# Attention on two lanes of 64 array rows, projections in halves, one PV run a unit

## The chip, the cores and the metric

The kernel runs on one core of a Trainium2 chip. TensorE multiplies (PE in the profile, PEld its weight loads), VectorE (DVE), ScalarE (ACT) and GpSimd (POOL) work on what it leaves, and SyncE (SP) starts the DMAs. Every engine takes its instructions in the order in which they were issued and waits for others by semaphores. The metric is the device time of one execution in microseconds; before, three runs gave a median of 1934.09 us (1932.29 to 1937.3).

## The reference

Two layers, each of an attention with a compressive memory and a gated feed-forward part, on x of 2048 rows and 512 columns. Cut to what matters:

```python
q, k, v = heads(x @ wq), heads(x @ wk), heads(x @ wv)   # 32 heads of 16, 4 segments of 512 rows
for s in range(4):
    logits = einsum("qd,kd->qk", qs, ks) * 0.25 + causal_mask
    a_dot = softmax(logits) @ vs
    a_mem = (phi(qs) @ M) / (phi(qs) @ z + 1e-6)        # phi(t) = t + 1 if t > 0 else exp(t)
    outs.append(g * a_mem + (1 - g) * a_dot)
    M, z = M + phi(ks).T @ vs, z + phi(ks).sum(rows)
x = x + concat(outs) @ wo                               # on layernorm(x)
x = x + (silu(h @ w_gate) * (h @ w_up)) @ w_down        # h = layernorm(x)
```

## The kernel before

The whole program is a list of operations. Each names its engine, a modelled cost, what it reads and writes, and a due time (`P.prio`, set by `at`). `Program.issue` (L148) then walks through modelled time and issues, on each engine, the due operation with the earliest due time whose inputs are there. So the order in every engine's queue is fixed when the kernel is built, by the planner's costs (`LAT`, `DRAIN`), its due times (`OFF`, `PRE`, `EP`) and the pitch of a unit (`TA`, `TF`). SyncE's queue is ordered in the same way.

Matrices are fp32r, one pass of the array. To keep precision the projections and the feed-forward part split each operand in a high and a low half and multiply three combinations (`mm3`, L285): 12 matmuls of 512 columns with 128 contraction rows for each 128x512 result. Its matmuls have line L282. PV, the memory and the transposes are plain fp32.

Attention runs over 32 units a layer: segment s, group n of eight heads, half h of four heads. For a unit:

- `load3` (L490) brings q and k of four heads from DRAM into `cq` and `ck`. The 48 contraction rows of a head (16 high, 16 low, 16 high) stand in a full-height operand among zeros.
- `mx_units` (L518): for each head the logits by query in groups of 256 + 256, 384 and 512 columns (L531). VectorE takes the maximum of each row (L538). `fin` transposes the maxima (L547), ScalarE negates them and a DMA writes them into `cq` as another contraction row (L550), so that the next product already has the maximum subtracted.
- `at_units` (L560): `lt` makes the logits by key, for two head pairs at once, ten tiles of 2 x 256 columns (L575). ScalarE takes the exp out of PSUM (L581), GpSimd masks the diagonal tiles (L585). `pv` multiplies with v on four lanes of 32 array columns (L603), in two runs. `post` drains (L616 to L637) and adds the part of the memory, whose transposes are L630.

Around this stand the projections of the next groups (`qk_proj`, `v_proj`, `wo_proj`), the layer norm with its transposes (`ln_transpose`, L370), phi (L475 to L480: Relu and Exp on ScalarE, the sum on VectorE), the reading of the memory (`mem_read`, L645) and its update (`mem_update`, L665, another run on column lanes). In the last units of a layer the first tiles of its feed-forward part are worked in (`up`, `down` and `ln` for blocks 0 and 1). The rest of that part works by Strassen's scheme (L987) and by `down` (L1042).

PSUM has eight banks, fixed by use: two `pmx` for maxima, three `plt` for the logits by key, one `ppv`, and two `pj` for all the rest, given out by the planner.

Of the kernel before, what the change touches and what calls it, by code (L numbers as in the profile page):

```python
# [26 lines left out]
WOT = ("pmx_0", "pmx_1", "pj", "pj")  # L27
# [4 lines left out]
WQ1 = -6.0  # L32
TA, TF = 15.0, 16.7
OFF = {'qe': (0.481, 1.468), 'at': (0.3, 1.1), 'mx': (-0.666, 0.16), 'lf': (-0.709, -0.318), 'mr': (0.865, 0.781), 'mu': (0.556, 0.139), 'wo': (0.263, 1.746), 'qk': (-0.342, 0.41), 'v': (-0.3, 0.518), 'lp': (0.034, 1.108)}
PRE = {'c': -1.851, 'mb': 0.212, 'lv': -1.7, 'lo': -0.87, 'gate': -1.0, 'v': -1.534, 'dv': 0.12, 'qk1': -1.2, 'mx': -1.0}
EP = {'w': -1.935, 'wn': 0.178, 'ln': -3.0, 'dn': -0.06, 'up': -2.73}
POOL_W = ""
TABLE = 1.28
DRAIN = {("full", "cols"): 0.195, ("cols", "full"): 0.095}
# [3 lines left out]
    pe=dict(pe=0.01, act=0.2, dve=0.2, sp=0.19),  # L43
# [7 lines left out]
class Buf:  # L51
    def __init__(self, prog, pool, tag, shape, dtype):
        self.prog, self.pool, self.tag, self.shape, self.dtype = prog, pool, tag, shape, dtype
        self.ops, self.left = [], 0
        self.w, self.r = {}, {}
        self.tile = None
        self.slot = None
# [10 lines left out]
class Op:  # L68
    __slots__ = ("table", "mode", "post", "eng", "cost", "lat", "fn", "prio", "bufs", "succ", "deps", "ready", "need", "wait", "index")

    def __init__(self, eng, cost, lat, fn, prio, bufs):
        self.eng, self.cost, self.lat, self.fn, self.prio, self.bufs = eng, cost, lat, fn, prio, bufs
        self.mode, self.table, self.post = None, None, 0.0
        self.succ, self.deps, self.ready, self.need, self.wait = [], set(), 0.0, None, 0


class Program:
# [3 lines left out]
    def __init__(self, shared):  # L81
        self.shared = shared
# [14 lines left out]
    def op(self, eng, cost, fn, reads=(), writes=(), lat=0.0):  # L97
# [38 lines left out]
        for b in touch:  # L136
# [3 lines left out]
            if b.tag in self.shared:  # L140
                o.need = b
# [6 lines left out]
    def issue(self):  # L148
        for b in {id(b): b for o in self.ops for b in o.bufs if b.tag in self.shared}.values():
# [9 lines left out]
        engs = sorted({o.eng for o in self.ops})  # L159
# [5 lines left out]
        held = {tag: [] for tag in self.shared}  # L165
        for o in self.ops:
            if o.wait == 0:
                heapq.heappush(fut[o.eng], (o.ready, o.index, o))
        done, bus, table, mode = 0, 0.0, "exp", "full"
        while done < len(self.ops):  # L170
            best = None
            for e in engs:
                f, n = fut[e], now[e]
                while True:
# [3 lines left out]
                    if n:  # L178
                        o = n[0][2]
                        b = o.need  # L180
                        if b is not None and b.slot is None:
                            if not free[b.tag]:
                                heapq.heappop(n)
                                held[b.tag].append(o)
                                continue
                            fr = min(free[b.tag])
# [5 lines left out]
                        start = t[e]  # L192
                    elif f:
                        start = f[0][0]
                        if best is None or start < best[0]:
                            t[e] = start
                            continue
                    else:
                        start = None
                    break  # L200
                if start is not None and n and (best is None or start < best[0]):
                    best = (start, e)
            assert best is not None, "no instruction can issue"
            start, e = best
            n = now[e]
            o = n[0][2]
            heapq.heappop(n)
            b = o.need
            if b is not None and b.slot is None:
                fr = min(free[b.tag])  # L210
                free[b.tag].remove(fr)
                b.slot = fr[1]
# [13 lines left out]
            end = t[e] + o.post  # L226
            if o.lat:
                bus = max(bus, end + 0.65) + o.lat
                end = bus
            for b in o.bufs:  # L230
                b.left -= 1
                if b.left == 0 and b.slot is not None:
                    free[b.tag].append((end + 0.25, b.slot))
                    for w in held[b.tag]:
                        w.ready = max(w.ready, end + 0.25)
                        heapq.heappush(fut[w.eng], (w.ready, w.index, w))
                    held[b.tag] = []
            for s in o.succ:
                s.ready = max(s.ready, end + LAT[e].get(s.eng, 0.0))
                s.wait -= 1  # L240
                if s.wait == 0:
                    heapq.heappush(fut[s.eng], (s.ready, s.index, s))
# [3 lines left out]
def infini_swiglu(ctx: ExitStack, tc: tile.TileContext, x, wq, wk, wv, wo, beta, wg, wu, wd, out,  # L246
# [8 lines left out]
    P = Program({"pj": 2})  # L255
# [5 lines left out]
    def bank(tag, ring=1):  # L261
        return P.buf(psum, tag, [128, 512], F32, ring)

    def pe(n, passes, fn, reads, writes, loads=1, mode="full"):
        o = op("pe", max(passes * n / 2400 + 0.0025 + 0.0145 * loads * (passes == 1), 0.11 * loads), fn, reads, writes)
        o.mode = mode
# [25 lines left out]


# [3 lines left out]
    amask = sb("amask", [128, 512], BF16)  # L297
    bsel = sb("bsel", [128, 4, 2])
# [71 lines left out]
    def ln_transpose(xn, xh, xl, t, tag="pj"):  # L370
        ps = bank(tag)
        for kc in range(KC):
# [6 lines left out]
            [ps, (xh, t)], [(xl, t)])  # L379

# [11 lines left out]
    SG = ("Y", "raw")  # L392

    CK = {}

    def attention(lay, x_in, x_out, slots, T, hook):
# [40 lines left out]
        def ln_fin(s, t, tag="pj"):  # L437
            if t == 0:
                xT[s] = (sb(S8["xh"], TX, F32R), sb(S8["xl"], TX, F32R))
            ln_transpose(XN.pop((s, t)), xT[s][0], xT[s][1], t, tag)  # L440

        def v_proj(s, t, tag="pj"):
            if s < 2 and t == 0:
# [5 lines left out]
            ps = bank(tag)  # L449
            c = slice(t * 128, (t + 1) * 128)  # L450
            mm3(ps, xT[s], W["v"], range(KC), lambda a, kc: a[:, t, kc], lambda a, kc: a[:, kc, :],
                lambda kc: t, lambda kc: kc, "a")
            vt = VT[s % 2]
# [4 lines left out]
        def qk_proj(s, n, nm, tag="pj"):  # L458
# [3 lines left out]
            ps, nat = bank(tag), g["nat"]  # L462
            a = 0 if nm == "q" else 1
            c = slice(n * 128, (n + 1) * 128)
            mm3(ps, W[nm], xT[s], range(KC), lambda t, kc: t[:, kc, c], lambda t, kc: t[:, :, kc],
                lambda kc: kc, lambda kc: None, "b")
# [739 lines left out]
```

## Time and profile before

| | before |
|---|---|
| median of three runs | 1934.09 us |
| the profiled execution | 1932.95 us |
| its span in the trace | 1931.2 us |
| granted TensorE clock, mean | 0.994 |
| layer 1: drains of the PV results, first to last | 77.6 to 534.3 us |
| layer 2: the same | 1037.9 to 1491.1 us |

The profile's page gives busy time by engine, the span in forty slices, the chain that ended last, and groups of instructions by line and tile. In a row of groups stand line, engine, operation, output and inputs, then the shapes and the count, then busy time and mean duration of one in ns, then the engine's idle time before them and what ended it. Matmuls are pipelined: one that starts 0.24 us after another may be shown as 0.4 us long. A row of windows has the stretch, its length, the busy time of each engine with its instructions, the granted clock, and the DMA engines' share and GB/s. A row of the timeline has start, length, engine, line, what is done, and how often in a row.

### The profile page before, as it was taken

To read this page: it belongs to the slowest core of one execution; us is meant where nothing else is said; L and a number is where in the kernel's file an instruction comes from. 1 tells how busy PE (TensorE), PEld (TensorE's weight loads), DVE (VectorE), ACT (ScalarE), POOL (GpSimd) and SP (SyncE) were. 2 spreads that over 40 slices of the span, in tenths; PEclk is the share of its full clock that TensorE was granted. 3 is DMA by queue.
4 is the path that set the end of the run, shared out by engine and by line. 5 is a ranking of instruction groups with operands and counts; after the bars stand their busy time and mean duration, and the time that the engine had idled before them with its cause. 6 is when DMAs were issued, how large, how long until landed. Compare 5 with 4: busy or idle time off the path is not lost.

```text
span 1931.2 us, 32319 instructions
## 1 busy us (share of the span) xinstructions
PE 1870.8 (97%) x11104; PEld 1437.2 (74%) x11104; DVE 1406.9 (73%) x3834; ACT 873.0 (45%) x1634; POOL 905.9 (47%) x1185
## 2 busy tenths in 40 slices
PE   7999999999989999999999999999999999999999
PEld 5677677776668887788867777777766788878887
DVE  5877867778777668766777678777797756686656
ACT  4555454555624343334326555555455334333332
POOL 5333443444546553655534334444355365455461
PEclk9999999999999999999999999999999999999999
DMA  7433434456131122221364344344561321221121
GB/s 235 135 111 124 132 116 146 129 151 195 45 136 50 55 72 82 71 61 44 95 215 121 102 133 132 116 149 132 152 188 39 131 66 44 87 77 51 44 60 44
DMA packets 120819, 206.09 MB, mean 107 GB/s; under 512 B 14160, under 2 KB 43856, under 8 KB 120656
## 3 DMA queue, kind: packets, MB, share of 16 engines
q1 hardware_dynamic: 118608, 203.49, 34.8%
q8 instruction: 89, 1.46, 0.3%
q10 hardware_dynamic: 2048, 0.53, 0.1%
q14 instruction: 74, 0.61, 0.1%
HBM read 136.34 MB, written 67.11 MB: 105 GB/s over the span
## 4 chain that ended last, share of the span: by engine, by line
PE 78%; DVE 8%; issue 4%; DMA 4%; POOL 3%; ACT 2%; SPq 0%; ACTq 0%; DVEq 0%; POOLq 0%
PE pj L282 16%; PE pj L1049 14%; PE plt L1005 11%; PE pmx L531 8%; PE pmx L1005 8%; PE ppv L603 7%; PE plt L575 6%; PE ppv L1005 3%; DVE junk L538 2%; DMA ck<-scrk 1%; PE pj L975 1%; PE pj L373 1%; PE pj L653 1%; DMA s<-nm 1%; POOL mem L858 1%
## 5 line engine op out<-in xcount | busy, mean ns | idle before, releaser
L538 DVE CUSTOM_DVE_ANT_0 junk<-pmx,amask 128x128 bf16<-128x128 f32 (+3 forms) x1024 | 458.7, 484 | 116.9 <-PE pmx L531 112.0
L282 PE MATMUL pj<-s,s 128*128 128x512 f32 x1416 | 488.2, 410 | 4.9 <-DVE s L1054 4.5
L1049 PE MATMUL pj<-s,vt 128*128 128x512 f32 x1296 | 414.4, 398 | 7.1 <-DVE s L1054 4.5
L581 ACT ACTIVATE s<-plt 128x512 f32<-128x512 f32 x512 | 284.2, 601 | 141.3 <-PE plt L575 133.3
L282 PEld LDWEIGHTS pj<-s,s 128*128 128x128 f32 x1416 | 263.9, 190 | 71.4 <-issue 24.9
L531 PE MATMUL pmx<-ck,s 127*128 127x256 f32 (+2 forms) x1024 | 299.1, 347 | 16.9 <-DVE mx L538 9.5
L1005 PE MATMUL plt<-s,s 128*128 128x512 f32 x1008 | 296.2, 396 | 3.4 <-ACT tt L1020 2.3
L1049 PEld LDWEIGHTS pj<-s,vt 128*128 128x128 f32 x1296 | 243.5, 189 | 68.9 <-DVE s L1054 8.0
L1054 DVE TENSOR_TENSOR s<-s,pj 128x512 f32<-128x512 f32 x224 | 152.9, 684 | 137.9 <-PE pj L1049 137.7
L575 PE MATMUL plt<-s,ck 128*128 128x256 f32 x1280 | 241.6, 288 | 4.2 <-DMA s<-nm 2.1
L531 PEld LDWEIGHTS pmx<-ck,s 127*128 127x128 f32 x1024 | 178.7, 190 | 88.8 <-DVE mx L538 27.0
L1005 PE MATMUL pmx<-s,s 128*128 128x512 f32 x720 | 239.2, 396 | 3.6 <-ACT s L871 2.4
L575 PEld LDWEIGHTS plt<-s,ck 128*128 128x128 f32 x1280 | 211.2, 189 | 32.7 <-ACT s L581 8.5
L1005 PEld LDWEIGHTS plt<-s,s 128*128 128x128 f32 x1008 | 189.6, 189 | 50.4 <-ACT tt L1020 2.7
L585 POOL TENSOR_SCALAR_AFFINE_SELECT s<-s 128x512 f32<-128x512 f32 x192 | 126.9, 664 | 186.5 <-ACT s L581 180.1
L1005 PEld LDWEIGHTS pmx<-s,s 128*128 128x128 f32 x720 | 135.5, 189 | 36.4 <-ACT s L871 3.2
L603 PE MATMUL ppv<-s,vt 128*32 128x512 f32 (+2 forms) x1536 | 136.8, 458 | 0.0
L872 POOL TENSOR_TENSOR s<-mem,s 128x512 fp32r<-128x512 f32 x96 | 126.4, 1318 | 0.0
L469 POOL TENSOR_SCALAR s<-raw 128x512 fp32r<-128x512 f32 x64 | 39.9, 624 | 181.0 <-ACT raw L468 180.6
L1005 PE MATMUL ppv<-s,s 128*128 128x512 f32 x288 | 112.8, 394 | 0.0
L879 POOL COPY turn<-vt 128x1 f32<-128x1 f32 x20 | 3.7, 184 | 230.0 <-DVE vt L962 230.0
L581 ACT ACTIVATE pc<-plt 128x512 f32<-128x512 f32 x128 | 76.8, 600 | 63.8 <-PE plt L575 62.5
(197 smaller groups left out, 2872.5 us busy)
## 6 DMA issues: line engine op xcount, KB each, us to landing
s<-scrq SPq DMA_DIRECT2D x128, 192.0 KB, 3.5
ck<-scrk SPq DMA_DIRECT2D x128, 192.0 KB, 4.5
scrq<-s SPq DMA_DIRECT2D x32, 512.0 KB, 3.0
scrk<-s SPq DMA_DIRECT2D x32, 512.0 KB, 3.1
scrq<-s SPq DMA_DIRECT2D x32, 256.0 KB, 2.0
scrk<-s SPq DMA_DIRECT2D x32, 256.0 KB, 2.0
xin<-xmid SPq DMA_DIRECT2D x32, 256.0 KB, 2.7
s<-xmid SPq DMA_DIRECT2D x32, 256.0 KB, 5.4
```

The lines of the kernel that those rows point to most:

```text
L282: pe(n, passes, lambda: nc.tensor.matmul(view(ps.ap), lhsT=av(a.ap), rhs=bv(b.ap), start=start, stop=stop), [(a, rk[0]), (b, rk[1])], [ps])
L469: gp(0.59, lambda: nc.gpsimd.tensor_scalar(out=nat.ap[:, a, 0, :], in0=raw.ap, scalar1=1.0, scalar2=0.0, op0=OP.mult, op1=OP.add), [raw], ...
L531: nc.tensor.matmul(ps.ap[:, a * 256:a * 256 + nk], lhsT=cq.ap[0:127, 2 * j + p, qt * 128:(qt + 1) * 128], rhs=ck.ap[0:127, p, 0:nk], start ...
L538: dve(w, lambda a=a, qt=qt, w=w, ps=ps, junk=junk: nc.vector.tensor_tensor_reduce(out=junk.ap[:, :w], in0=ps.ap[:, a * 256:a * 256 + w], i ...
L575: nc.tensor.matmul(ps.ap[:, 256 * p:256 * p + 256], lhsT=ck.ap[:, p, kt * 128:kt * 128 + 128], rhs=cq.ap.rearrange("r (j p) c -> r p j c", ...
L581: act(512, lambda: nc.scalar.activation(Pb.ap[:, x].rearrange("p i c -> p (i c)"), ps.ap, AF.Exp, scale=SCALE), [ps], [(Pb, x)], table="exp")
L585: gp(0.593, lambda: nc.gpsimd.affine_select(out=Pb.ap[:, x], in_=Pb.ap[:, x], pattern=[[0, 4], [1, 128]], compare_op=OP.is_ge, fill=0.0, b ...
L603: nc.tensor.matmul(ps.ap[32 * i:32 * i + 32, q0:q0 + w], lhsT=vt.ap[:, kt, VW * hd:VW * hd + 32], rhs=f_[sl].ap[:, b0:b0 + w // 128, idx], ...
L872: gp(n / 400, lambda hi=hi, lo=lo, src=src: nc.gpsimd.tensor_sub(lo(), src(), hi().bitcast(F32)), [read, (wt, (o0, 0))], [(wt, (o0, 1))])
L1005: pe(512, 1, lambda i=i, kc=kc, x=x, buf=buf, view=view: nc.tensor.matmul(ps.ap, lhsT=w.ap[:, o, i, kc], rhs=view(buf.ap, kc), start=(x == 0),
L1049: pe(512, 1, lambda i=i, j=j, fi=fi, x=x, ps=ps, wt=wt, cs=cs: nc.tensor.matmul(ps.ap, lhsT=ht.ap[:, 0:2048].rearrange("p (f a c) -> p f a ...
L1054: dve(512, lambda ps=ps, t=t: nc.vector.tensor_add(xb.ap[:, t, :], xb.ap[:, t, :], ps.ap), [ps, (xb, t)], [(xb, t)])
```

## The change

- The contraction rows of two heads are put into the array's halves: head j of a pair lies in rows 64j to 64j + 48 of one tile `c3`, and its products use 64 array rows (mode "rows", lane j). The maxima are the same twelve groups of columns a unit, six on each lane. The logits by key become twelve groups of their own, one head each, with key tiles 3 and 2 together (256 + 256), 1 (384) and 0 (512). The exps follow these shapes, the masks take two diagonal tiles of one head at once, and the negated maxima go out in two DMAs.
- The planner keeps a queue of its own for each lane. Between full array, row lanes and column lanes it counts a switch (`DRAIN`).
- Projections in attention and the early feed-forward tiles come in pairs (`duo`). Each product is cut into two halves of 64 contraction rows, one on each lane, both accumulating in the same bank. So that both lanes don't write a bank at once, SyncE executes an empty instruction between: it waits for the first half's last matmul, and the second half's first matmul waits for it.
- PV is one run a unit after all exps, and a memory update joins the run.
- Transposes of maxima, layer norm (two tiles at once), memory and keys, and the reading of the memory go in two lanes; their results come in two banks. For layer norm pairs ScalarE copies twice and GpSimd subtracts, in place of VectorE.
- All eight banks are shared; the planner gives them out, with limits by kind (`CAP`).
- phi's sum is taken from VectorE: ScalarE makes a second Relu, GpSimd adds. `post` multiplies by the gate and by the reciprocal in one instruction.
- The due times and `TA` are others. `raw` has two buffers, `junk` one.

The core of the diff:

```diff
-TA, TF = 15.0, 16.7
+TA, TF = 13.54, 16.7
+CAP = {"mx": 2, "lt": 2, "dn": 2, "g": 3, "u": 3}
-    P = Program({"pj": 2})
+    P = Program({"bank": 8}, CAP)
+    ROWS = (slice(0, 64), slice(64, 128))
+    def halves(ps, seq, lane, n=512):
+        done, gate_, z = [], [], None
+        for half, ln_ in enumerate((lane, 1 - lane)):
+            for x, (view, lhsT, rhs, reads) in enumerate(seq):
+                def fill(half=half, x=x, view=view, lhsT=lhsT, rhs=rhs, r=ROWS[ln_]):
+                    ins = nc.tensor.matmul(view(ps.ap, r), lhsT=lhsT(r), rhs=rhs(r), start=half == 0 and x == 0,
+                                           stop=half == 1 and x == len(seq) - 1)
+                    if half == 0 and x == len(seq) - 1:
+                        done.append(ins)
+                    if half == 1 and x == 0:
+                        behind(ins, gate_[0])
+                o = pe(n, 1, fill, reads, [ps], mode="rows", lane=ln_)
...
+            if half == 0:
+                def let():
+                    gate_.append(nc.sync.nop())
+                    behind(gate_[0], done[0])
+                z = op("sp", 0.05, let)
...
+    def duo(X, Y):
+        halves(*X, 0)
+        return halves(*Y, 1)
+    def turn(units, reads):
+        A = [bank(), bank()]
+        for i, (r, ps) in enumerate(zip(ROWS, A)):
+            for out, in_ in units:
+                pe(64, 2, lambda out=out, in_=in_, r=r, ps=ps: nc.tensor.transpose(out(ps.ap), in_(r), ident.ap[r, r]),
+                   reads + [ident], [ps], mode="rows", lane=i)
...
+            act(512, lambda pv=pv, rv=rv: nc.scalar.copy(rv(), pv()), [ps], [xn])
+            gp(1.25, lambda rv=rv, out=out: nc.gpsimd.tensor_sub(out(xl), rv(), out(xh).bitcast(F32)),
+               [xn] + keys(xh), keys(xl))
...
-                dve(512, lambda: nc.vector.scalar_tensor_tensor(out=ph.ap, in0=raw.ap, scalar=0.0, in1=ph.ap,
-                                                                op0=OP.max, op1=OP.add), [raw, ph], [ph])
+                act(512, lambda: nc.scalar.activation(raw.ap, raw.ap, AF.Relu), [raw], [raw], sbuf=True)
+                gp(1.25, lambda: nc.gpsimd.tensor_add(ph.ap, ph.ap, raw.ap), [raw, ph], [ph])
...
+        def mx_group(u, p, j, grp):
...
+            mx, ps, r = f_["mx"], bank("mx"), slice(64 * j, 64 * j + 48)
+            mms = [lambda a=a, qt=qt, nk=max(256, 128 * (qt + 1)): nc.tensor.matmul(
+                ps.ap[:, a * 256:a * 256 + nk], lhsT=c3.ap[r, p, qt * 128:(qt + 1) * 128],
+                rhs=c3.ap[r, 2 + p, 0:nk], start=True, stop=True) for a, qt in enumerate(grp)]
...
+        def lt_group(u, p, j, k, grp):
...
+            mms = [lambda kt=kt, c0=c0, w=w: nc.tensor.matmul(
+                ps.ap[:, c0:c0 + w], lhsT=c3.ap[r, 2 + p, kt * 128:kt * 128 + 128],
+                rhs=c3.ap[r, p, 512 - w:512], start=True, stop=True) for kt, c0, w in grp]
...
+        MXG = ((0, 1), (2,), (3,))
+        LTG = (((3, 0, 256), (2, 256, 256)), ((1, 0, 384),), ((0, 0, 512),))
+        def lane(u, x, kind):
+            p, y, j = x // 6, x % 6 // 2, x % 2
...
+            pe(n, 1, lambda: [m() for m in mms], reads, [ps], loads=len(mms), mode="rows", lane=j)
+        def pv_run(u, mu=None):
...
+                for x, (kt, q0, w, part, o) in enumerate(((0, 0, 512, 0, 0), (1, 128, 384, 0, 512), (3, 384, 128, 1, 0),
+                                                         (2, 256, 256, 1, 128))):
+                    for idx in range(4):
...
+                if mu:
+                    for t in range(4):
+                        for i in range(4):
...
```

More of the change, by code (lines that the diff above doesn't have):

```diff
@@ L148, in issue @@
     def issue(self):
-        for b in {id(b): b for o in self.ops for b in o.bufs if b.tag in self.shared}.values():
+        for b in {id(b): b for o in self.ops for b in o.bufs if b.tag in self.shared and b.kind not in ("g", "u")}.values():
             first = b.ops[0].index
@@ L226, in issue @@
             end = t[e] + o.post
+            if e == "pe":
+                for x in ("lane0", "lane1") if o.lane is None else (q,):
+                    t[x] = t[e]
+                t["pe"] = max(t["lane0"], t["lane1"])
             if o.lat:
@@ L488, in attention @@
         C3 = {}
+        PA, PC = [], []
         def load3(u):
@@ L990, in strassen @@
             (h0, l0), (h1, l1) = XT[2 * m], XT[2 * m + 1]
-            PX, PY, PZ = [bank(t) for t in (("plt_0", "plt_1", "plt_2") if nm == "g" else ("ppv", "pmx_0", "pmx_1"))]
+            PX, PY, PZ = [bank(nm) for _ in range(3)]
             C, V = {}, {}
```

645 lines of the change are left out of this document (371 added, 274 removed).

## The prediction, made before the result was known

> **What bounds the kernel now.** I read the page first: the share of each engine, the forty slices, the chain that ended last.
>
> ```profile
> span 1931.2 us, 32319 instructions
> PE 1870.8 (97%) x11104; PEld 1437.2 (74%) x11104; DVE 1406.9 (73%) x3834; ACT 873.0 (45%) x1634; POOL 905.9 (47%) x1185
> PE   7999999999989999999999999999999999999999
> PEclk9999999999999999999999999999999999999999
> PE 78%; DVE 8%; issue 4%; DMA 4%; POOL 3%; ACT 2%; SPq 0%; ACTq 0%; DVEq 0%; POOLq 0%
> ```
>
> TensorE is nearly full in all slices but the first and the one around 540 us, where attention ends, its clock is full, and 78% of the chain is its own work. So an edit is worth the TensorE time that it takes away, until another engine is as full. The change edits attention, so I cut the first layer at the drains of the PV results (L616): segment 0, segments 1 and 2, segment 3, then the feed-forward part.
>
> ```profile
> core 0: us, PE busy (x) PEld busy (x) DVE busy (x) ACT busy (x) POOL busy (x), PEclk, DMA share, GB/s
> 77.60:183.80 106.20, 105.92 (x843) 79.87 (x842) 81.23 (x315) 61.41 (x122) 44.15 (x66) 1.00 0.41 120
> 183.80:433.40 249.60, 244.72 (x1875) 183.03 (x1874) 187.47 (x704) 128.73 (x253) 103.09 (x155) 1.00 0.45 133
> 433.40:541.00 107.60, 100.34 (x673) 71.94 (x671) 84.33 (x267) 56.84 (x104) 55.38 (x82) 1.00 0.39 116
> 541.00:970.00 429.00, 419.94 (x1813) 336.94 (x1814) 303.76 (x479) 161.63 (x288) 228.31 (x257) 0.99 0.25 77
> ```
>
> A unit (two passes over four heads) takes 106.2/8 = 13.28 us in segment 0, 249.6/16 = 15.6 in segments 1 and 2, and 107.6/8 = 13.45 in segment 3, with TensorE 93 to 100% busy. VectorE works 10.15, 11.7 and 10.5 us of each unit: 76, 75 and 78%. The feed-forward part keeps its matmuls, so I leave its 429 us alone.
>
> **The logits in two lanes.** The prices are read from starts that follow each other in the timeline of TensorE, since a matmul's length there holds its pipeline's tail.
>
> ```profile
> 185.45 0.40 PE L575 MATMUL plt<-s,ck 128*128 128x256 f32 x2
> 185.69 0.40 PE L282 MATMUL pj<-s,s 128*128 128x512 f32 x1
> 185.93 0.40 PE L531 MATMUL pmx<-ck,s 127*128 127x256 f32 x2
> 186.16 0.40 PE L282 MATMUL pj<-s,s 128*128 128x512 f32 x1
> 186.40 0.34 PE L531 MATMUL pmx<-ck,s 127*128 127x384 f32 x1
> 186.58 0.39 PE L282 MATMUL pj<-s,s 128*128 128x512 f32 x1
> ```
>
> A pair of 256 columns or one product of 512 takes 0.24 us, one of 384 takes 0.18. Before, a unit's maxima (L531) are four heads of 0.24 + 0.18 + 0.24 = 0.66, so 2.64 us, and its transposed logits (L575) ten pairs, 2.40. After, both are twelve groups of those three sizes, six on each lane: 2 x 0.66 = 1.32 for each kind if two lanes run side by side. That takes 5.04 - 2.64 = 2.40 us off a unit. No trace of before has a 64-row lane. The bounds: nothing gained (lanes in turn, 5.28 us) and the full 2.40. The nearest row is that of the four column lanes of PV:
>
> ```profile
> L603 PE MATMUL ppv<-s,vt 128*32 128x512 f32 x512 | 68.2, 605 | 0.0
> L1005 PE MATMUL plt<-s,s 128*128 128x512 f32 x1008 | 296.2, 396 | 3.4 <-ACT tt L1020 2.3 <-ACT s L940 0.5 <-DVE tt L1018 0.4
> ```
>
> 512 x 605 ns = 310 us of matmul stand in 68.2 busy us, 4.5 at a time; in a full-height group 1008 x 396 ns stand in 296.2, 1.35 at a time. So lanes by column do overlap, and I take the full 2.40.
>
> **One PV run.** The array's shape is switched around each run:
>
> ```profile
> 255.90 0.42 PE L282 MATMUL pj<-s,s 128*128 128x512 f32 x1
> 256.25 1.07 PE L603 MATMUL ppv<-s,vt 128*32 128x384 f32 x16
> 257.13 0.61 PE L603 MATMUL ppv<-pc,vt 128*32 128x256 f32 x8
> 257.68 1.65 PE L282 MATMUL pj<-s,s 128*128 128x512 f32 x6
> ```
>
> The first product should end its slot 0.24 after 255.90, and the run starts 0.11 later. Its 16 records (384 and 128 columns) take 0.88 to the next row, so the last 256 columns should take 0.44, and the next product starts 0.11 later than that. The two switches cost 0.22. One run fewer in each unit saves 0.22, and the memory update that joins the run another 0.22 in each of 12 groups a layer. Bounds: 0 (the new switch, rows to columns, may cost twice) and 0.44. In total a unit gets 2.62 us shorter on TensorE, 2.73 where it has half an update, and the memory read in two lanes (12 groups) gives between nothing and half of L653's busy time, 0.75 a group; I take 0.4, so 0.2 a unit. Transposes are as many instructions on each lane as before on the array: nothing. TensorE's pace, if nothing else came in, would be 13.28 - 2.73 = **10.55**, 15.6 - 2.93 = **12.7** and 13.45 - 2.82 = **10.6** us: 22 + 47 + 22 = 91 us a layer.
>
> **Projections half by half.** Per layer 32 pairs of products (14 of q and k, 6 of v, 6 of wo, 4 early gate and up, 2 early down). Each pair has 48 matmuls of 512 columns, 24 on a lane: 24 x 0.24 on both lanes at once, which is the 2 x 12 x 0.24 = 5.8 us of before. So no gain, and a new wait: the second half of a product may not start until SyncE has seen the first half end, and TensorE's queue behind it stands still, the other lane's work included.
>
> ```profile
> 246.85 0.34 PE L531 MATMUL pmx<-ck,s 127*128 127x384 f32 x1
> 247.22 0.56 DVE L538 CUSTOM_DVE_ANT_0 junk<-pmx,amask 128x384 bf16<-128x384 f32 x1 [0.36 <-PE pmx L531]
> ```
>
> A waiting engine starts 0.37 us after a product of 0.18, so 0.2 after its slot; SyncE's step and the way back come on top. Between 0 (logits of the other unit fill it) and about 0.6 a pair I take 0.45, uncovered and once, since both lanes change together: 32 x 0.45 = 14 us a layer.
>
> **The other engines.** What goes over to ScalarE and GpSimd, and what VectorE loses:
>
> ```profile
> L478 DVE SCALAR_TENSOR_TENSOR phik<-raw,phik 128x512 f32<-128x512 f32 x28 | 22.4, 799 | 2.5 <-ACT phik L476 2.5
> L378 DVE TENSOR_TENSOR s<-pj,s 128x512 fp32r<-128x512 f32 x60 | 39.9, 679 | 6.6 <-ACT s L377 6.5
> L618 DVE TENSOR_SCALAR r<-r,gnot 128x16 f32<-128x16 f32 x64 | 16.0, 249 | 1.2
> L471 POOL TENSOR_TENSOR s<-raw,s 128x512 fp32r<-128x512 f32 x64 | 84.3, 1317 | 3.8
> L581 ACT ACTIVATE s<-plt 128x512 f32<-128x512 f32 x512 | 284.2, 601 | 141.3 <-PE plt L575 133.3
> L475 ACT ACTIVATE phik<-raw 128x512 f32<-128x512 f32 x28 | 17.7, 633 | 1.7 <-DVE s L383 1.4
> ```
>
> phi's sum leaves VectorE: 24 a layer at 0.8, of which 6, 14 and 2 fall into the three stretches, 0.6, 0.7 and 0.2 us a unit. The scaling of r goes (0.25 a unit). The subtraction behind the transposed layer norm goes for the tiles taken in pairs (0.34 a unit, 0.68 in segment 3, where early feed-forward tiles are paired too). The split addition of the memory part costs about 0.08. The 16 reductions of a unit stay. VectorE is left with 9.0, 10.5 and 9.45 us a unit. ScalarE, 128.7/16 = 8.0 now, gets the second Relu (0.63 x 14/16), exps of other widths (at most 12 x 0.6 for 10 x 0.6) and copies of the pairs: about 10. GpSimd, 6.4 now, gets phi's sum and the pairs' subtraction at 1.32 each, 1.8 together; the masks keep their elements. About 8.3. Neither is the fullest engine, and TensorE's work ahead covers them; without that cover each late exp holds one of only two logits banks.
>
> VectorE is another matter: at TensorE's pace it would be busy 9.0/10.55 = 85%, 83% and 89%, and it must empty two banks of maxima, one while the other is filled. No attention stretch of before shows it above 78%. I take that as its ceiling, so a unit takes no less than 9.0/0.784 = 11.5, 13.4 and 12.05 us. The gain is then 8 x 1.8 + 16 x 2.2 + 8 x 1.4 = 61 a layer, less 14 for the hand-overs: 47, or **94 us** in both. From this execution's own 1932.95 us (span 1931.2 and 1.75 around it; the median of the runs is 1934.09, 0.06% above) that gives **1839 us**. Bounds of this case: 1800 with hand-overs covered and VectorE at 80 to 85%, 1865 with 0.6 a pair and switches that cost what they saved.
>
> **Rivals.** *TensorE alone decides.* VectorE keeps up at 85 to 90%: 2 x (91 - 14) = 154, so 1779, and 1751 with hand-overs hidden. For it speaks that before TensorE lost only 9.5 us in total to VectorE; against it, that VectorE then had a quarter of its time free.
>
> ```profile
> PE pmx L531 <- DVE mx L538: 9.5, 23, 1.1
> SPq L483 <- POOL s L469: 310.6, 54, 11.6
> ```
>
> *SyncE is late.* The step between halves stands in the queue that starts the DMAs. There L483's starts wait for GpSimd, 310.6/54 = 5.8 us each. Where a step is queued behind such a start, both lanes stand for the rest of that wait. If a quarter of the 64 pairs lose half of it, 16 x 2.9 = 46 us: 1885.
>
> *The loads of the two lanes queue.* Each lane loads its own weights, twice as many loads as before. By L575's pitch, 0.12 for a product with its load, four loads take 0.48 where a pair of two-part groups should take 0.24, and two take 0.24 against 0.18: 4 x 0.24 + 4 x 0.06 = 1.2 us a unit, 77 in all; partly under VectorE's ceiling, so 1860 to 1915.
>
> [...]
>
> *Lanes by row overlap badly, and the kernel gets slower.* The work meant for two lanes is 32 x 2.64 + 32 x 5.8 = 270 us a layer, at 0.24 for a pair. At p it costs 270 x (p/0.24 - 1) more, against 47 gained: it decides from p = 0.28 us. With no overlap (p = 0.48) projections double: 32 x 5.8 = 186 a layer lost against the gain of the runs only, about 2290. This is also the case in which the change doesn't do what it says. Against it stands L603's row, for it only that the row shows lanes by column.
>
> [...] No run so far shows a row lane.
>
> **How the numbers follow.** My forecast (1800 to 1865) gets 50%, TensorE alone (1745 to 1800) 16%, SyncE late (1865 to 1925) 12%, queued loads 10%, bad overlap 9%; 3% for gains and losses that cancel. The range 1760 to 1905 holds the first, most of the second and more than half of the third and fourth: 8 in 10. A measurement here tells 0.3%, 6 us, from no change: faster 0.88, within 0.03, slower 0.09.
>
> **What would show it.** In the timeline, logits of the two lanes start a few ns apart and a pair of 512 takes 0.24 us (right) or 0.28 and more (bad overlap). One PV run of 32 records a unit instead of one of 8 and one of 24. VectorE in segments 1 and 2 near 78%; at 85% or more TensorE alone decided. Waits of TensorE on SP near 0.45 us; several us mean the SyncE rival. What would make me wrong first is the ceiling, a number read from stretches in which VectorE never had to be faster.

## The result, and the profile after

The changed kernel takes 2027.32 us (median of four runs, 2019.95 to 2029.8) against 1934.24: ratio 1.0473, 95% interval 1.0442 to 1.0505. It is 93 us slower, where 94 us less were forecast, and far outside the range. The page of the execution after:

```profile
span 2027.1 us, 36966 instructions
PE 1931.9 (95%) x12944; PEld 1469.8 (73%) x12944; DVE 1411.3 (70%) x3706; ACT 944.8 (47%) x1938; POOL 1055.2 (52%) x1526
PE   7999999999999999999998999999998999999999
PEclk9599898798799999999998988998988999999999
PE 58%; DVE 8%; issue 4%; POOL 3%; DMA 2%; ACT 2%; ACTq 0%; SPq 0%; DVEq 0%; POOLq 0%
```

TensorE looks as full as before. The row of the clock has changed: in more than half of attention's slices it shows 8 or less, where before it was 9 throughout. The views of the cores give a mean clock of 0.936 instead of 0.994. As the clock's records have only two values here, full and half, the time at half clock is 2 x (1 - clock) x span: 259 us after, and 25 before (by the records themselves; the rounded clock gives 23).

The windows of the first layer, cut at the drains of PV (L757 after): segment 0, segments 1 and 2, segment 3, then feed-forward, then attention of layer 2. Columns as before: length, busy time of PE, PEld, DVE, ACT and POOL, then the clock.

```profile
84.90:194.60 109.70, 104.56 (x1024) 73.12 (x1025) 78.44 (x296) 69.27 (x156) 59.45 (x105) 0.94 0.38 106
194.60:468.90 274.30, 261.44 (x2440) 195.01 (x2442) 184.18 (x683) 147.19 (x333) 140.73 (x248) 0.89 0.43 126
468.90:587.50 118.60, 109.31 (x794) 75.84 (x796) 74.38 (x250) 63.56 (x130) 63.20 (x109) 0.81 0.36 99
587.50:1096.60 509.10, 490.36 (x2236) 390.34 (x2236) 368.51 (x627) 191.28 (x347) 266.54 (x300) 0.99 0.29 89
1096.60:1571.20 474.60, 448.12 (x4190) 324.69 (x4192) 336.30 (x1215) 278.14 (x618) 262.34 (x457) 0.91 0.43 121
```

(The limits in the prediction and the drains in the table before it were counted from the trace's zero, 11.03 us ahead of the span's start, so those windows lie 11 us late. The windows from the drains themselves, at 66.5, 172.8 and 422.4 to 523.2, give VectorE 77, 75 and 79%; the third is 100.8 us long, 12.6 a unit and not 13.45. Nothing in the argument turns on it.)

A unit of segments 1 and 2 takes 274.3/16 = 17.1 us, not 13.4, and VectorE is at 67%, below its share of before. From the first drain to the last, attention takes 502.6 and 474.6 us, where it took 456.7 and 453.3: 67 of the 93 us. Of the rest some 18 lie ahead of the first unit's drain, where 34 us run at half clock.

How the clock falls is seen in windows of 3.41 us: the 66 clock records of this trace begin whole multiples of 3.41 us apart. Here are four stretches of the kernel after, around one fall:

```profile
227.80:234.60 6.80, 6.65 (x105) 4.80 (x105) 6.48 (x26) 3.68 (x9) 5.34 (x9) 1.00 0.69 218
234.62:238.03 3.41, 2.73 (x21) 2.19 (x22) 3.15 (x13) 2.50 (x6) 1.95 (x6) 1.00 0.57 186
238.03:248.27 10.24, 8.66 (x41) 5.12 (x45) 7.69 (x33) 3.63 (x9) 6.64 (x14) 0.50 0.60 118
248.27:255.10 6.83, 5.93 (x68) 3.58 (x60) 5.00 (x18) 4.64 (x11) 3.05 (x6) 1.00 0.07 18
```

In the second, TensorE is shown busy for 2.73 of 3.41 us, 80%, and VectorE for 3.15. Then the clock is halved for three windows. What TensorE did in that window, from its timeline (L676 are the logits by key, L642 the maxima, L791 the reading of the memory, L369 transposes; L335, further below, are the halves of projections):

```profile
234.60 0.68 PE L676 MATMUL bank<-s 49*128 49x512 f32 x2
235.22 0.46 PE L369 MATMUL bank<-ident,mem 64*128 64x64 f32 x4
235.51 0.61 PE L791 MATMUL bank<-mb,phiq 64*128 64x68 f32 x4
235.86 0.49 PE L676 MATMUL bank<-s 49*128 49x512 f32 x1
235.97 0.38 PE L791 MATMUL bank<-mb,phiq 64*128 64x68 f32 x2
236.16 0.41 PE L676 MATMUL bank<-s 49*128 49x384 f32 x1
236.41 0.33 PE L791 MATMUL bank<-mb,phiq 64*128 64x68 f32 x2
236.83 0.47 PE L642 MATMUL bank<-s 48*128 48x256 f32 x2
237.89 0.43 PE L642 MATMUL bank<-s 48*128 48x256 f32 x1 [0.59 <-DMA s<-scrk]
237.90 0.49 PE L676 MATMUL bank<-s 49*128 49x256 f32 x1
```

Small products on 48 to 64 rows, one or two at a time. Over the whole trace the clock falls 33 times. In 29 of the windows ahead of a fall, those in attention and its start, no product is on the full array of 128 rows and 128 output columns, and TensorE is shown busy for 0.33 to 0.99 of the window, median 0.75. Of the 480 windows that kept full clock 209 hold no product on the full array either; there it is shown busy for 0.71 or more, median 1.00. So the busy share alone doesn't part the two.

The texts on record below also give how full a window is, as a share of the array (0.25, 0.38). That is the author's estimate from this trace, matmul time weighted with the rows and output columns in use. No run measures the weights, and no limit is shown: by that estimate every window ahead of a fall holds 0.38 or less, but so do six that kept the clock, the lowest at 0.30.

Whatever halves the clock is called the gate from here on. The first theory after this: **with few rows in use the clock falls, attention on lanes uses few, and half clock costs the time**. Its rivals: gaps alone make it fall; or half clock falls only in time that is waiting anyhow, and the lanes starve for another reason.

### The profile page after: what moved, and what is told of

The parts are those of the page before. It is cut to its first block, busy times and chain, and to the rows that moved or that the text cites. A ratio compares the mean times of both kernels' runs of the same rounds, so it can differ in the third digit from the quotient of the medians.

```text
span 2027.1 us, 36966 instructions
## 1 busy us (share of the span) xinstructions
PE 1931.9 (95%) x12944; PEld 1469.8 (73%) x12944; DVE 1411.3 (70%) x3706; ACT 944.8 (47%) x1938; POOL 1055.2 (52%) x1526
## 4 chain that ended last, share of the span: by engine, by line
PE 58%; DVE 8%; issue 4%; POOL 3%; DMA 2%; ACT 2%; ACTq 0%; SPq 0%; DVEq 0%; POOLq 0%
PE bank L1176 22%; PE bank L1228 14%; PE bank L335 9%; PE bank L735 5%; DVE junk L649 4%; PE bank L676 3%; PE bank L642 3%; PE bank L311 1%; DMA s<-nm 1%; POOL mem L1019 1%; PE bank L369 1%; POOL s L1033 1%; PE bank L791 1%; POOL xn L446 1%; DVE s L1107 0%
## 5 line engine op out<-in xcount | busy, mean ns | idle before, releaser
L335 PE MATMUL bank<-s,s 64*128 64x512 f32 x2880 | 608.0, 421 | 4.6 <-SPq L346 2.9
L649 DVE CUSTOM_DVE_ANT_0 junk<-bank,amask 128x256 bf16<-128x256 f32 (+3 forms) x1024 | 500.1, 488 | 138.2 <-PE bank L642 41.1
L1176 PE MATMUL bank<-s,s 128*128 128x512 f32 x2016 | 484.2, 398 | 14.9 <-ACT s L1106 6.0
L1176 PEld LDWEIGHTS bank<-s,s 128*128 128x128 f32 x2016 | 379.9, 190 | 109.4 <-ACT s L1106 7.8
L335 PEld LDWEIGHTS bank<-s,s 64*128 64x128 f32 x2880 | 423.4, 196 | 45.2 <-SPq L346 7.6
L642 PE MATMUL bank<-s 48*128 48x256 f32 (+2 forms) x1024 | 305.3, 395 | 21.9 <-DVE mx L649 15.3
L676 PE MATMUL bank<-s 49*128 49x256 f32 (+2 forms) x1024 | 293.1, 385 | 20.0 <-DMA s<-nm 7.3
L1228 PE MATMUL bank<-s,vt 128*128 128x512 f32 x1248 | 297.0, 395 | 2.5 <-ACT vt L1127 1.3
L1228 PEld LDWEIGHTS bank<-s,vt 128*128 128x128 f32 x1248 | 233.7, 188 | 58.7 <-DVE vt L1128 2.3
L642 PEld LDWEIGHTS bank<-s 48*128 48x128 f32 x1024 | 177.3, 206 | 82.2 <-DVE mx L649 23.1
L686 ACT ACTIVATE s<-bank 128x384 f32<-128x384 f32 (+1 forms) x344 | 177.7, 547 | 90.7 <-PE bank L676 48.1
L676 PEld LDWEIGHTS bank<-s 49*128 49x128 f32 x1024 | 168.5, 200 | 68.0 <-DVE mx L649 16.7
L757 DVE STREAM_TRANSPOSE tt<-bank 128x512 f32<-128x512 f32 x64 | 45.8, 716 | 124.5 <-PE bank L735 124.5
```

Of the source, the lines that this page charges most:

```text
L335: ins = nc.tensor.matmul(view(ps.ap, r), lhsT=lhsT(r), rhs=rhs(r), start=half == 0 and x == 0, stop=half == 1 and x == len(seq) - 1)
L642: mms = [lambda a=a, qt=qt, nk=max(256, 128 * (qt + 1)): nc.tensor.matmul(ps.ap[:, a * 256:a * 256 + nk], lhsT=c3.ap[r, p, qt * 128:(qt + ...
L649: dve(w, lambda a=a, qt=qt, w=w: nc.vector.tensor_tensor_reduce(out=junk.ap[:, :w], in0=ps.ap[:, a * 256:a * 256 + w], in1=amask.ap[:, 512 ...
L676: mms = [lambda kt=kt, c0=c0, w=w: nc.tensor.matmul(ps.ap[:, c0:c0 + w], lhsT=c3.ap[r, 2 + p, kt * 128:kt * 128 + 128], rhs=c3.ap[r, p, 51 ...
L686: act(512 if kt == 0 else 384, lambda: nc.scalar.activation(out(), src(), AF.Exp, scale=SCALE), [ps], [(buf, key)], table="exp")
L757: dve(512, lambda: nc.vector.transpose(ta.ap.rearrange("p a b -> p (a b)"), ps.ap), [ps], [ta])
```

## The experiments

**What makes the clock fall** (gate). A kernel of its own, dense stages between warm stretches:

```diff
+    def both(rows, n):
+        for _ in range(n):
+            one(bank[0], 0, rows)
+            one(bank[1], 64, 64 + rows)
...
+    def paced(lo, hi, w, n):
+        for i in range(n):
+            ps = bank[3 + i % 2]
+            one(ps, lo, hi)
+            nc.vector.tensor_copy(res[:, 0:w], ps[:, 0:w])
```

`one(ps, lo, hi)` is a product of 512 columns on rows lo to hi; `lane` repeats it on the first lane alone.

> No part of the reference is computed: stages of fp32r matmuls of 512 columns alone, between warm stretches of 150 full-height ones, to read the granted clock. The changed kernel's windows of 3.41 us at full clock were followed by half clock when matmul time x rows / 128 was 0.38 of the window or less, and kept it from 0.42 up; with the share of time in which any matmul ran the two sets overlap (0.49 to 0.61). Theory A (the gate weighs activity by the rows in use): one lane of 64 rows (0.46) keeps 1.0; one lane of 48 rows (0.35) is at the edge and should fall; one lane of 32 rows (0.23) falls; both lanes of 32 (0.46) keep 1.0; both lanes of 48 behind a fallen stage (0.70 to 0.75) are at the edge of coming back, both of 64 come back in one window; full-height matmuls paced by VectorE reading 512 columns (0.31) fall, by 256 columns (0.5) stay, and 64 rows at that same pace (0.25) fall. Theory B (only gaps in time count): no dense stage falls, whatever its rows; of the paced ones the two at 256 columns behave alike.

The windows of this kernel: one lane of 64 rows (the first row), one lane of 48, both of 48, one of 32, both of 32, and the paced stages of 128 rows at 256 columns and 64 rows at 256.

```profile
42.00:84.00 42.00, 42.00 (x187) 34.09 (x186) 0.00 (x0) 0.00 (x0) 0.00 (x0) 1.00 0.00 1
120.00:202.00 82.00, 82.00 (x201) 62.59 (x200) 0.00 (x0) 0.00 (x0) 0.00 (x0) 0.52 0.00 0
240.00:283.00 43.00, 43.00 (x384) 35.52 (x382) 0.00 (x0) 0.00 (x0) 0.00 (x0) 1.00 0.00 1
451.00:508.00 57.00, 57.00 (x143) 43.63 (x142) 0.00 (x0) 0.00 (x0) 0.00 (x0) 0.53 0.00 0
581.00:624.00 43.00, 43.00 (x384) 35.28 (x382) 0.00 (x0) 0.00 (x0) 0.00 (x0) 1.00 0.00 1
742.00:793.00 51.00, 48.30 (x98) 18.06 (x98) 41.01 (x98) 0.00 (x0) 0.00 (x0) 1.00 0.00 0
829.00:891.00 62.00, 61.91 (x96) 26.64 (x95) 40.63 (x96) 0.00 (x0) 0.00 (x0) 0.51 0.00 0
```

The second row decides: 82 us without a gap on one lane of 48 rows ran at a mean clock of 0.52, so 79 of them (2 x 0.48 x 82) at half. One lane of 64 rows, 187 products in 42 us, kept 1.00. The two paced stages are the same program but for the rows: full-height products, 98 in 51 us, ran at 1.00, those on 64 rows, 96 in 62 us, at 0.51. So in these stages the rows in use made the difference, and gaps alone don't explain it. Gaps made one too: full-height products paced by reads of 512 columns, 56 in 44 us, ran at clock 0.52. All that theory A expected of this kernel came. Both lanes of 48 rows, straight behind one lane of 48 at half clock, brought it back: from 380.00 to 414.00 the mean clock was 0.95, some 3.4 us at half. The third row also gives the price of the lanes: 384 products in 43 us, 0.224 us for a pair, what a single lane takes for one (187 in 42, 0.225). In this stage two lanes by row overlapped fully. In the kernel after they do so with 256 columns and a load for each product too: the four of the first row take 0.24 us to the next.

```profile
85.11 0.41 PE L676 MATMUL bank<-s 49*128 49x256 f32 x4
85.35 0.40 PE L335 MATMUL bank<-s,s 64*128 64x512 f32 x1
```

No idle window came before these falls: TensorE was shown busy for 80% of the window in the kernel's case above, and for all of the 82 us of the second row.

**More rows for the logits** (k64, lt64). In k64 both kinds of logits use 64 rows, with a DMA that zeroes row 48 ahead of the maxima:

```diff
-            mx, ps, r = f_["mx"], bank("mx"), slice(64 * j, 64 * j + 48)
+            mx, ps, r = f_["mx"], bank("mx"), slice(64 * j, 64 * j + 64)
-            ps, r = bank("lt"), slice(64 * j, 64 * j + 49)
+            ps, r = bank("lt"), slice(64 * j, 64 * j + 64)
+                    dma(lambda j=j: nc.sync.dma_start(c3.ap[64 * j + 48:64 * j + 49, 0:2].bitcast(F32),
+                                                      c3.ap[64 * j + 50:64 * j + 51, 0:2].bitcast(F32)), ...
```

> The changed kernel with the logits' matmuls of both kinds on 64 rows of each lane in place of 48 and 49; the added rows of q are zero, and a small DMA per lane and unit sets row 48 back to zero before the maxima. Columns, order of the planner's matmuls and lanes stay, two short DMA starts a unit are added on SyncE. Theory A (half clock because few rows are in use): the logits weigh a third more, so the time at half clock falls from 262 us to about 100 to 170 and the time from 2027 to about 1950 to 1990. Theory B (gaps in time): rows do nothing, 262 us stay and the time is 2027 or up to 15 more for the DMA starts.

2045.92 us, 1.0566 [1.0548, 1.0585], clock 0.933: a miss for theory A, half clock wasn't shortened (274 us). It came out nearly as theory B had it, 4 us above its range. lt64 leaves the DMAs out and widens the logits by key alone:

> The changed kernel with 64 rows in use in place of 49 for the logits by key alone; the added rows of q are zeros from a memset, no DMA is added (the earlier run with 64 rows for both kinds, 2046 us and 276 us at half clock, had two DMA starts a unit more on SyncE). Theory A with recovery: the gate's falls come from windows with little work of any kind (median 0.25 of the array), which a third more weight on half of the logits doesn't lift over 0.38, so half clock stays at 200 to 280 us and the time within 2005 to 2035. Rival (the added DMA starts spoiled the earlier run, rows in the logits do decide): half clock below 170 us, time below 1995.

2027.92 us, 1.0473 [1.0446, 1.0499], clock 0.937. The same as the changed kernel, as the theory with recovery had it. More rows in the logits by key alone left half clock at 2 x 0.063 x 2025.2 = 255 us. That fits windows ahead of a fall that hold little work of any kind (TensorE shown busy for 0.75 of them, the median above).

**What half clock costs** (bank7, fill7, fill33). Seven shared banks; in fill7 and fill33 the eighth takes 878 extra products on lane 0, where the planner leaves it empty. fill33 differs from fill7 in rows only:

```diff
-    P = Program({"bank": 8}, CAP)
+    P = Program({"bank": 7}, CAP)
+        nc.tensor.matmul(fb, lhsT=w[0:64, 0:128], rhs=w[0:64, 0:512], start=True, stop=True)   # fill7
+        nc.tensor.matmul(fb, lhsT=w[0:33, 0:128], rhs=w[0:33, 0:512], start=True, stop=True)   # fill33
```

> The changed kernel with seven shared PSUM banks in place of eight; the control for the next run. All theories: somewhat slower than 2027, 2040 to 2090, since banks come free later; half clock at least as long as 262 us.

> Seven shared banks, and in the eighth 878 extra matmuls of 64 rows and 512 columns whose result nobody reads, placed on lane 0 where the planner leaves that lane without work in attention (about 200 us of lane time). Theory A: windows that stood at 0.25 gain up to 0.3, so most of the half clock goes (below 60 us), and the time is 80 to 130 below that of the control. If half clock isn't what costs the time (rival: waits for VectorE and banks cost it, and the clock only falls in time that was idle anyhow): the clock comes back but the time stays within 20 us of the control.

> The run with extra matmuls on lane 0 again, at the same places and of the same length, but with 33 rows in use in place of 64, so that they weigh half as much for the gate. TensorE's time for them is the same; what differs from the 64-row run (2076 us, clock 0.964) is the clock alone. Theory A (half clock costs about half of the time that it lasts while matmuls run): clock falls to about 0.94 to 0.95, the time rises by 15 to 50 us to about 2090 to 2125. Rival (the clock falls only where TensorE waits anyhow, so it costs nothing): clock falls, time stays at 2076 within 10.

bank7 took 2075.86 us (one run, clock 0.931), fill7 2076.15 (one run), fill33 2141.57, 1.1029 [1.0974, 1.1085]. Their views of the cores, fill7 first:

```profile
core 0: 2074.4 us, clock 0.964
```

```profile
core 0: 2144.8 us, clock 0.923
```

Half clock is 2 x 0.036 x 2074.4 = 149 us and 2 x 0.077 x 2144.8 = 330. By itself fill7 looked like the rival's case: more clock (bank7 has 2 x 0.069 x 2074.1 = 286 us at half clock), no less time. But it holds lane 0 for 878 products, and fill33 holds it for as many. Between these two only the rows in use differ, and 181 us more of half clock took 70 us more, 0.39 each; that is more than the 15 to 50 expected, since the clock fell further. The other three runs of fill33, with 118 to 168 us more than fill7, give 0.39 too. So half clock costs time, and fill7's gain was eaten by its own products. For the changed kernel, 234 us more than before at 0.39 are some 91 us. That is an estimate from this pair, in which fill7 has one run: no kernel here has the changed attention at full clock throughout. Runs of one and the same kernel go along with it: the changed kernel's slowest and fastest are 2027.8 us at clock 0.936 and 2017.9 at 0.942, 10 us for 25 more at half clock.

**Why it would not be faster at full clock either** (paired, pairduo, fullproj). With these estimated 91 us taken off, 1936 are left, about the time before, and not the 1839 of the forecast. By an estimate, at full clock in attention (each product as long as its columns at 2.4 a ns, twice the 1.2 of half clock, where products of 512 columns start 0.427 us apart in the trace of before; plain fp32 twice as long) both lanes stream in 39% of the time, one alone in 27%, none in 18%, PV's columns in 15%. (Some of the 27 and 18% lies between products that follow each other without a wait: in the stage on one lane of 64 rows they start every 0.225 us, where 512 columns at 2.4 a ns are 0.213.) paired issues the logits' groups of both lanes as one entry of the planner, pairduo the projections' halves too, fullproj takes the halves back:

```diff
+            if j:
+                return
+            pe(n, 1, lambda: [m() for ms in zip(*[g[1] for g in G]) for m in ms], G[0][2] + G[1][2],
+               [G[0][0], G[1][0]], loads=len(G[0][1]), mode="rows")
...
-                    put([lambda g_=g_: qk_two(g_ // 4, g_ % 4)], ...
+                    put([lambda g_=g_, nm=nm: qk_proj(g_ // 4, g_ % 4, nm) for nm in "qk"], ...
```

> The changed kernel with the logits' groups of both lanes issued together, lane by lane in turn, so that they start and end side by side; each needs two banks at once. In the changed kernel one lane ran alone in 27% of attention's time at full clock. Theory one-lane (lanes drifting apart cost half of that time, 60 us a layer): one lane alone falls to 15 to 20%, the time to about 1960 to 2000. Rival (banks and VectorE starve the lanes anyhow): what one lane alone loses comes back as time with no lane at work, and the time is 2030 to 2090, as the two banks at once wait longer.

> As the run before, and the projections' halves too are issued pair by pair for both lanes, so that no lane works alone but in transposes and memory reads. Theory one-lane: one lane alone below 8%, the time 1920 to 1980. Rival (starved by banks and VectorE): no lane at work rises by as much as one lane alone falls, the time is 2030 to 2100.

> The changed kernel with the projections and the early feed-forward tiles undone: full-height products as before, no halves, no SyncE step; logits, memory and transposes stay on two lanes, so the array changes shape far more often. If the halves are what costs (waits for SyncE, lanes drifting apart): faster than 2027, about 1950 to 2000. If the halves cost next to nothing (11 us of waits of TensorE for SyncE in the trace): slower, since each change of shape costs 0.1 to 0.2 us and the logits can no longer run beside a projection; 2060 to 2200.

paired 2071.04 (one run), pairduo 2107.25, 1.0883 [1.0866, 1.0901], fullproj 2252.81 (one run, clock 0.872). In paired one lane alone rose to about 31%, so it tests little. In pairduo it fell from 27% to 16 to 18%, and no lane at work rose from 18 to 25%: the rival's picture, with a time a little above its range, as half clock rose to 2 x 0.093 x 2107.3 = 392 us. So issuing the lanes side by side doesn't win back what one lane alone loses; both wait. Taking the halves back doesn't help either: fullproj is 225 us slower, more than either theory allowed. But its half clock is 2 x 0.128 x 2251.1 = 576 us, 317 more, which at 0.39 is 124 of the 225, and its array changes shape more often, so it doesn't price the halves by themselves. How little TensorE waits for SyncE shows in the waits of the kernel after, whose columns are who waited for whom, us in total, times, longest:

```profile
PEld bank L335 <- SPq L346: 8.2, 13, 3.4
PE bank L335 <- SPq L346: 3.1, 2, 2.9
```

**Who starves the lanes** (lightdve, lightact, phidve).

```diff
-                        out=junk.ap[:, :w], in0=ps.ap[:, a * 256:a * 256 + w], in1=amask.ap[:, 512 - w:],
+                        out=junk.ap[:, :64], in0=ps.ap[:, a * 256:a * 256 + 64], in1=amask.ap[:, 512 - w:576 - w],
```

> The changed kernel, but each of the 1024 reductions for the maxima reads 64 columns in place of 128 to 512, so VectorE leaves out four fifths of them: some 6.6 us of a unit become about 3. The order of all queues stays. Theory VectorE (the lanes starve since VectorE empties the banks of maxima too slowly, and the gate follows): one lane alone and no lane at work fall from 27% and 19% to below 20% and 15%, half clock to below 100 us, the time to 1850 to 1920. Rival (ScalarE's exps, or the order of the queue itself, hold the lanes): the time falls by less than 40 us, half clock stays above 200 us.

> The changed kernel, but each exp reads 128 columns in place of 384 or 512 (the rest of its tile holds ones from a memset at the start of a layer): ScalarE's 6.4 us of exps a unit become about 3.4. Theory VectorE: the time falls by less than 40 us. Rival ScalarE (two banks for the logits by key, emptied by ScalarE, hold the lanes): one lane alone falls below 20%, the time to 1850 to 1930. If neither of the two light runs gains 40 us: the order in which the queue was laid out holds the lanes.

lightdve took 1970.8 us (one run, clock 0.94), lightact 2027.15 (one run). ScalarE's exps are not the limit: with 128 columns in place of 384 or 512 (0.49 and 0.60 us each in the changed kernel), they change nothing. VectorE's reductions are a part of it. Their groups, after (four forms in the page's row) and in lightdve:

```profile
L649 DVE CUSTOM_DVE_ANT_0 junk<-bank,amask 128x256 bf16<-128x256 f32 (+3 forms) x1024 | 500.1, 488 | 138.2 <-PE bank L642 41.1
```

```profile
L649 DVE CUSTOM_DVE_ANT_0 junk<-bank,amask 128x64 bf16<-128x64 f32 x1024 | 228.1, 223 | 271.2 <-PE bank L642 157.7
```

272 us less of VectorE's work bought 56 us of time. That is less than the theory's 107 to 177 and more than the rival's 40, and half clock stayed at 2 x 0.06 x 1968.9 = 236 us, as the rival had it. No lane at work fell from 18 to 14%, one lane alone stayed at 27%. So VectorE's reductions hold a part, and neither they nor the exps hold the rest. That it is the order in the one queue, which both lanes share, fits, but no run isolated it. The banks are another candidate: bank7, with one fewer, is 49 us slower than the changed kernel, of which 26 us more at half clock explain about 10. No run gave the maxima or the logits by key a third bank.

phidve puts phi's sum back on VectorE:

```diff
-                act(512, lambda: nc.scalar.activation(raw.ap, raw.ap, AF.Relu), [raw], [raw], sbuf=True)
-                gp(1.25, lambda: nc.gpsimd.tensor_add(ph.ap, ph.ap, raw.ap), [raw, ph], [ph])
+                dve(512, lambda: nc.vector.scalar_tensor_tensor(out=ph.ap, in0=raw.ap, scalar=0.0, in1=ph.ap, ...
```

> The changed kernel with phi's sum back on VectorE, one instruction in place of the second Relu on ScalarE and the sum on GpSimd. Alone in the kernel before, moving it off cost 12 us. Theory VectorE (its time starves the lanes, the run with light reductions gained 56 us for some 3.6 us less of its time a unit): 0.7 us a unit more on VectorE cost about 10 to 20 us, 2035 to 2050. Rival (what phi's readers wait for is the longer chain over ScalarE and GpSimd): 5 to 15 us faster, 2010 to 2022.

2058.45 us, 1.063 [1.0609, 1.0651], clock 0.918: 31 us slower than with the sum on GpSimd, more than the 10 to 20 expected. Half clock rose to 2 x 0.082 x 2058.2 = 338 us, 79 more, which at the 0.39 of the pair above is all of the 31. That a later VectorE leaves TensorE less to do at a time, and half clock then makes the price, fits this, but it rests on that 0.39.

**Two parts of the change alone, in the kernel before** (onepv, phipool). One PV run a unit with full-height logits, and phi's sum on GpSimd:

```diff
-                    parts = PARTS[k]
+                    parts = PARTS[0] + PARTS[1]
...
-            units = [lt(0, q) for q in range(4)] + [lt(1, q) for q in (1, 2, 3)] + [pv(0)]
+            units = [lt(0, q) for q in range(4)] + [lt(1, q) for q in (1, 2, 3)]
```

> The kernel before with one part of the change alone: both PV runs of a unit are one, after all exps; full-height logits, no lanes by row. If a run's two switches are worth 0.22 us as read from the timeline: 64 x 0.22 = 14 us less, 1915 to 1925. Rival (the single buffers of the exps are held to the end of the unit, so the next unit's exps and logits wait): same or slower, 1935 to 1990.

> The kernel before with another part alone: phi's sum on GpSimd after a second Relu on ScalarE. VectorE is not what bounds the kernel before, so all theories say no change: 1928 to 1940.

onepv 1941.74, 1.0034 [1.0023, 1.0045]; phipool 1947.2, 1.0063 [1.0048, 1.0079]. Neither gains there. One run a unit costs 7 us where 14 less were expected, in the range of its rival, exps' buffers held longer; that this is the reason was not isolated. phi's sum on GpSimd costs 12 us where it was expected to be free. That relieving VectorE gains nothing there fits a kernel that TensorE bounds; the sum's longer way over two engines, with `raw` in one buffer, may be what costs, but no run shows it. No kernel tried beats the one before.

## Why the prediction was wrong, by its steps

- **"Its clock is full [...] So an edit is worth the TensorE time that it takes away."** This step failed. The clock was read as a given, and no rival had it. It is an outcome of the schedule: its mean went from 0.994 to 0.936, and 29 of the 33 falls came in the changed attention and its start, behind windows without a product on the full array. By the fill7 and fill33 pair some 91 us of the miss of 188 are the price. The saving that was sought puts products on half the array's rows or fewer, and a lone stage on 48 rows ran at 0.52 where one on 64 kept 1.00; more rows for the logits alone (k64, lt64) didn't undo it, at 0.933 and 0.937.
- **"So lanes by column do overlap, and I take the full 2.40."** Right as to the overlap, though read from another kind of lane: 0.224 us for a pair of 48 rows in the lone stage, so the rival of bad overlap fell. Queued loads fell with the four products of 256 columns in 0.24 us, where that rival needs 0.48.
- **VectorE's 78%: "I take that as its ceiling".** This step failed too. VectorE reached 67% in segments 1 and 2, and a unit took 17.1 us, not 13.4. The sum took the busy shares of engines for the limit, so that lanes standing empty far below any ceiling had no term. VectorE has a hand in it (56 us for 272 us of its work). The other 97 us of the miss are not the clock's by that estimate; what holds the part that VectorE doesn't, the order of the queue, the banks or something else, stays open. For the rival without a ceiling the prediction said that TensorE lost 9.5 us in total to VectorE; that is the row of the maxima alone, and all its rows of matmuls together come to 25 us.
- **Hand-overs, 14 us a layer.** Too high: TensorE waited at most 11 us in both layers for SyncE. The rival of a late SyncE is refuted.
- **One PV run, 0.22 us a unit saved.** Not seen: alone it cost 7 us in the kernel before. What it does inside the changed kernel wasn't tried.
- **phi's sum costs nothing.** Wrong both ways: 12 us lost in the kernel before, 31 us gained in the changed one.
- **The slower side** had a chance of 0.09 and one mechanism, which isn't the one that came. And the test named last, VectorE's share, pointed below the ceiling, where the text had looked for trouble only above it.

## What to carry to other kernels

The granted clock of before is not to be carried into a forecast for a change that puts products on fewer rows: here its mean went from 0.994 to 0.936, and the 234 us more at half clock cost some 91 us by the estimate above. Run a lone stage with the rows and the pace that are planned first and read its clock, as with 48 and 64 rows here (0.52 and 1.00). Less TensorE work pays only if something else fills the time. TensorE's busy share doesn't see an empty lane (95% here), so count both lanes.

## What the runs showed of the hardware

- In the kernel of lone stages, products of 512 columns without a gap ran at these mean clocks: one lane of 64 rows 1.00 over 42 us, of 48 rows 0.52 over 82 us, of 32 rows 0.53 over 57 us; both lanes of 48 rows and both of 32 rows 1.00, over 43 us each.
- Paced by VectorE, full-height products ran at 1.00 with 98 in 51 us and at 0.52 with 56 in 44 us, products on 64 rows at 0.51 with 96 in 62 us.
- Behind one lane of 48 rows at half clock, both lanes of 48 brought it back, with some 3.4 us at half in their 34 us (mean clock 0.95). In the changed kernel half clock lasted 34.1 us at its longest, ahead of the first unit's drain.
- In the changed kernel the mean clock was 0.94, 0.89 and 0.81 in the stretches of layer 1's attention, 0.91 in layer 2's, and 0.99 in the feed-forward part between, where 1932 of 2234 products are on the full array; in those stretches of attention 24 of 8441 are.
- Two row lanes of 48 rows ran 384 products of 512 columns in 43 us, twice as many as one lane of 64 rows ran in that time (187 in 42).
